# Six sums of squares of weights on VectorE, the high halves of GpSimd's splits on GpSimd, and a new order, in a fused attention and MLP kernel

## The chip, the cores and the metric

The kernel runs on one core of a Trainium2 chip. The metric is the device time of one execution in microseconds, taken as the median of several runs. The profiler also records one execution with a trace of every engine: TensorE (PE, with its weight loads PEld), VectorE (DVE), ScalarE (ACT), GpSimd (POOL) and SyncE (SP), which here only issues transfers.

## The reference, cut to what matters

```python
xn = _layernorm(A_x)                                  # 2048 tokens x 512
return x + _A_ref(xn, wq, wk, wv, wo, beta) + _B_ref(xn, w1, b1, w2, b2)

def _A_ref(x, ...):            # 32 heads of 16, 4 segments of 512 tokens
    q, k, v = x @ wq, x @ wk, x @ wv
    for s in range(4):
        a_dot = softmax(qs @ ks^T * scale + causal mask) @ vs
        a_mem = (phi(qs) @ M) / (phi(qs) @ z + 1e-6)   # phi(t) = t + 1 if t > 0, else exp(t)
        o = g * a_mem + (1 - g) * a_dot
        M += phi(ks)^T @ vs ; z += sum(phi(ks))
    return o @ wo

def _B_ref(x, ...):
    return gelu(layernorm(x) @ w1 + b1) @ w2 + b2      # 512 -> 1792 -> 512
```

## The kernel before

All large products are made in three f16 matmuls instead of one f32 matmul: each operand is split into a high half (the value, scaled and rounded to f16) and a low half (what rounding left over), and the products high x high, high x low and low x high are added in PSUM (`split3`, L480). A weight's scale is a power of two that is found on the chip from the weight's sum of squares. So each group of weights ("qk" is the first group of heads of wq and wk, "QK" the other three groups, "v", "1a" and "2a" the first halves of w1 and w2, "1b" and "2b" the second halves, "o" is wo) goes through four steps before TensorE can use it:

- `w_load` (L252 to L280): transfers into the place where the f16 halves will stand later, or into a borrowed tile (`pt`, `acc`, `oT`, `rc`, `ame`). All are issued on SyncE.
- `w_square` (L311): one ScalarE activation for each piece, which squares it and leaves the row sums in a column of `am`.
- `w_scale` (L326, L343 to L357): TensorE adds the row sums over the partitions by a matmul with `ones`; ScalarE takes a root through Ln and Exp (L320, L321), and VectorE cuts it to a power of two and inverts it.
- `w_split`: each 128x512 piece is split either the "V" way (ScalarE writes the high half, L366, and VectorE the low half, L367) or the "G" way (GpSimd scales the piece in place, L369, ScalarE copies it to f16 as the high half, L370, GpSimd subtracts the two for the low half, L371). The table `SPLIT` says which piece goes which way; 21 pieces go the G way.

The work is cut into 16 items of one segment and one group of 8 heads. For each item: the projections of k and q (`T`, L480, then L514 to L530), which go through DRAM (`kd`, `qd`) into stacked tiles `kst` and `qst`; row maxima of the logits (`M`: matmuls L621, VectorE L628; `R` writes them out to DRAM and back into `qst`); exponentials (`S`: matmuls L661, ScalarE L666, the causal mask on GpSimd L675); the product with v (`pv`, L690); normalisation (`O`, L698 to L726); the memory terms (L536 to L607). The MLP is 16 steps: hidden products (`D`, L480 with w1s, brought out by L756), gelu (`G`, L763), the split of the result (`H`, L770 on GpSimd, L771 on ScalarE, L772 on GpSimd) and the second product (`e`, L797, added by L803). `out` (L815, L818) is the last projection. There are also 14 `warm` steps of eight matmuls of `ones` with itself (L828), whose results are used by nothing.

No scheduler decides the order: every engine runs its own instructions in program order, and the program order is written out. `streams()` lists the steps of each kind in sequence, and the string `ORDER` names, letter by letter, which stream gives the next step. `BANKS` gives each new PSUM tile its bank in the same way. Both strings were found by a search.

Of the kernel before, what the change touches and what calls it, by code (L numbers as in the profile page):

```python
# [56 lines left out]
def streams():  # L57
# [31 lines left out]
    for m in PARTS:  # L89
# [10 lines left out]


ORDER = (
    "aatcucuccvavtctveecttcetcuvaactvuvtaatcattavdtubcwwvccfwxxcxwxyxyxxgyhxcoxxvwxofooowcvwzyzoiyyiazgyyziiynzoiiys"
    "ppAnziiniicvzvcniiooAzmAihiiopzqqiqcivpqjpqjijqqijizqjiqqjiiAwszBzoAskkkkmjiAojoijsoAijAqjqjasAfoAopgkkkkpjpjqq"
    "jlpoolojjjooilihAAkkkkpaiqqiqijqjqqijqjiqjqjisBfgpiiqkkkkmpliqqiooiqpBlqoBopohijjiojiijpolsjiqaqajqiqiqqiiqapka"
    "kmkktspaqijqiqjqiqajqbqajopijjgBfopkkkBkjjjlooooBlhjjjolqiqqiipkkkkjiqqijqqjjiqiqjjqiqiqiBkkkkmpliilfnplimpngrr"
    "mrjjponijqjqjinjipiskmkkmkaiijrijjoojiqsjqqjiqiiiqqkkkkihlqlfmlogojqjqjqqjjasoojmkkkkmqjiqjqjjaojjpipmooisikkkk"
    "lpilhiofmgoooqiqpppqiqiqqqiiiqqpsosmoiqqiiqiqppsslooijqjojijojijoiaakkkkmpaijqjqjaqqqjiqqjiqjqiikmkkakbqiaqqahl"
    "olfqjjojqmjgjjoolmmkkkkmhjjoojjiitjiojiippkkkkliiilnfnimpligniinipmrrijjrsijqjqiqjiqjqiipkmkkksiqjqijqjqjiqjqii"
    "qjqikmpkkkiprlqsphlfojmjgopjjlojpjoomokmkkkqiqisjojiqisjqiqijqqijqhiqqiiqjsqiiqppmkkkkilalofomqpgopaoooospmlajq"  # L110
    "qqjqqjqjqiiqiqqqjqiqqipipooooiijooppoiaakkkkmajiqpisqqjiqjqjaiqaqhjqqqjqaaqmkkkkbjlfoljqjmjgojjqolmkkkkmmjjjooj"
    "jioijoiiippkpkkkiinliifniiilnnimlgrpmjjrmjjjrrijikkpskkiqqijqiqijqqjiqjiqjqiqjiqiispqkpkskksqilqoplfojmjgjjjpoo"
    "oojolmkkkkiqjiqpsjiqiqijqjqiqijqjiqiqiqiiqqkksmkpikplolfjjqmjgjjjoooooklpkmkkjiiopjqiqijqjiqpjqiqijqiqqiqiiqikk"
    "pspkkqiplpoooopljjjqqqjqjjqooolkpskmkpkmqqqpqjpjqqqjqjqpqqjqjqqqkmkkkqlllqqqqqqqqqrrrr"
)

BANKS = (
    "012345670123457063571265407321640573216405732164053271640527163054271630542713605427105472105427105472105472015"  # L120
    "470251407251405712470512470512470536124075631254076340125637123756123576132576132576132576132576135402761350427"
    "163054273106542736574326574326537425632754632574631072456310724563071245360712453620731620731067203617621073621"
    "073621073621037621037621037261702361475023671540263701524603175246031746013746013713460713471630471630463714067"
    "314056723410523674105236741052367410527410527410527410527410527140352671450326475103264751023674523674523647253"
    "647236547236475264735264107532410765324107265431067512043675120436751204736152047361520473615270346150312750317"
    "250317253107250371257013275027135027134650132754062751340621375460376054370567403056374065374065307645307645307"
    "642153076241076241076241076253410762534621075346210754316024310264310432610432610324610324612403246013752640163"
    "754207156437120564371205647312056473120564731206547321065473265104723607423460273460273642073642073642051736420"
    "157642031765420316750316705315631705630157630157630157306173504621357462017345620147536210436024136024316403216"
    "403216403216403216740536740536740536740536271406"  # L130
)


# [14 lines left out]
def infini_mixer_kernel(ctx: ExitStack, tc: tile.TileContext, x, wq, wk, wv, wo, beta, w1, b1, w2, b2, out):  # L148
    nc = tc.nc
    V, A, G, T, Q = nc.vector, nc.scalar, nc.gpsimd, nc.tensor, nc.sync  # L150
# [136 lines left out]
    def w_square(m, k):  # L287
        if m in ("qk", "QK"):
            w, g = part(m, k)
            r, junk, to = piece(w, g), WT[w][:, 1], am[:, NG * "kq".index(w) + g:NG * "kq".index(w) + g + 1]  # L290
        else:
            to = am[:, AM[m] + k:AM[m] + k + 1]
            a = m[0]
            if m == "1a" and k == 2:
                r, to = b1t, am[:, 16:17]
            elif m[1:] == "a":
                r = flat(a)[:, 1024 + 1792 * k:2816 + 1792 * k]
            elif m[1:] == "b":
# [12 lines left out]
        A.activation(junk.bitcast(BF)[:, :r.shape[1]], r, AF.Square, accum_out=to)  # L311

    def floor2(dst, src):
# [45 lines left out]
    def w_split(m, n):  # L359
        w, c = part(m, n)  # L360
        s = qkcol(1, "kq".index(w), c) if w in "kq" else \
            col({"v": SV, "o": SO, "1": S1, "2": S2}[w] + (m[1:] == "b"))
        r = piece(w, c)
        h, l = WT[w][:, c, 0, :], WT[w][:, c, 1, :]
        if SPLIT[m][n] == "V":
            A.activation(h, r, AF.Copy, scale=s)  # L366
            V.scalar_tensor_tensor(l, r, s, h, op0=OP.mult, op1=OP.subtract)  # L367
        else:
            G.tensor_scalar(r, r, s, 0.0, op0=OP.mult, op1=OP.add)  # L369
            A.activation(h, r, AF.Copy)  # L370
            G.tensor_tensor(l, r, h, op=OP.subtract)  # L371

    wqs, wks, wvs, wos, w2s = (WT[m] for m in "qkvo2")
# [487 lines left out]
    def once(kind, n, make):  # L861
# [49 lines left out]
```

## Time and profile before

| | |
|---|---|
| median of 3 runs | 695.24 us (695.22 to 695.28) |
| the profiled execution, its time | 694.85 us |
| its span, first to last instruction | 693.1 us |
| mean granted TensorE clock | 0.995 |
| busy: PE / DVE / ACT / POOL | 678.7 / 535.4 / 522.7 / 347.2 us |
| ScalarE busy, 10 to 40 us from the start | 29.09 of 30 us |
| TensorE busy, 20 to 30 us | 5.41 of 10 us |

Times in the profile are counted from the first instruction of the span. A row of a timeline gives the start, the duration and the engine, then the line, the operation, what is written and read, and in brackets the idle time of the engine before it with what ended that idle time. A row of the windows view gives the length of a stretch, the busy time of PE, PEld, DVE, ACT and POOL in it with their numbers of instructions, the granted TensorE clock as a share of the full one, the share of the DMA engines and GB/s.

### The profile page before, as it was taken

What the parts mean: (1) busy time and instruction counts of PE and PEld (TensorE: products, weight loads), DVE (VectorE), ACT (ScalarE), POOL (GpSimd) and SP (SyncE); (2) the same over time, 40 slices, a digit from 0 to 9 for tenths busy, and PEclk for the clock granted to TensorE, in tenths of its full rate; (3) what the DMA queues carried; (4) which work ended last, traced back from release to release, by engine and by line L of the source; (5) the groups of instructions that cost most, each with busy time, mean ns of one, the idle gap of its engine ahead of it and who ended that gap; (6) DMA issues with size and microseconds to landing.
All of it is one profiled execution on the core that took longest, in us unless ns stands there. A gap on an engine that the chain in (4) does not pass through costs nothing.

```text
span 693.1 us, 16949 instructions
## 1 busy us (share of the span) xinstructions
PE 678.7 (98%) x6359; PEld 395.7 (57%) x6359; DVE 535.4 (77%) x1695; ACT 522.7 (75%) x1013; POOL 347.2 (50%) x533
## 2 busy tenths in 40 slices
PE   7799999999999999999999999999999999999997
PEld 6465556576654555566554456567564456656653
DVE  4499978897795887998798786888678595969442
ACT  5989898878795659857795697757795687778870
POOL 5276768365624425664334445454362546455752
PEclk9899999999999999999999999999999999999999
DMA  9984222420204213431113224231120416140101
GB/s 272 283 238 136 64 63 63 108 62 14 84 10 115 87 44 74 100 71 33 51 45 92 63 72 99 63 93 33 31 80 24 132 18 152 18 108 3 18 1 61
DMA packets 51790, 55.12 MB, mean 80 GB/s; under 512 B 4782, under 2 KB 40636, under 8 KB 51708
## 3 DMA queue, kind: packets, MB, share of 16 engines
q1 hardware_dynamic: 49404, 49.84, 25.3%
q0 software_dynamic: 2304, 4.20, 3.7%
q8 instruction: 50, 0.82, 0.5%
q14 instruction: 32, 0.26, 0.1%
HBM read 36.99 MB, written 17.04 MB: 78 GB/s over the span
## 4 chain that ended last, share of the span: by engine, by line
PE 78%; ACT 10%; POOL 4%; DVE 3%; issue 2%; DMA 1%; SPq 1%; POOLq 0%; ACTq 0%; DVEq 0%
PE ps L480 33%; PE ps L797 16%; PE ps L690 10%; PE ps L815 6%; PE ps L661 5%; PE ps L621 5%; ACT pt L666 2%; DVE ps L628 2%; PE ps L571 2%; PE ps L499 1%; ACT hT L763 1%; ACT hT L771 1%; SPq L252 1%; POOL w1s L371 1%; DMA pt<-in_A_wk_dram 1%
## 5 line engine op out<-in xcount | busy, mean ns | idle before, releaser
L628 DVE CUSTOM_DVE_ANT_0 ps<-ps,mask 128x512 f32<-128x512 f32 (+3 forms) x512 | 233.8, 522 | 16.1 <-PE ps L621 14.9
L666 ACT ACTIVATE pt<-ps,qkcs 128x512 f32<-128x512 f32 (+1 forms) x384 | 206.1, 624 | 35.3 <-PE ps L661 33.5
L797 PE MATMUL ps<-w2s,hT 64*128 64x512 f16 x1344 | 176.7, 376 | 0.2
L480 PE MATMUL ps<-xnT,w1s 128*128 128x256 f16 x1344 | 157.8, 273 | 0.0
L675 POOL TENSOR_SCALAR_AFFINE_SELECT pt<-pt 128x256 f32<-128x256 f32 x256 | 99.1, 414 | 92.0 <-ACT pt L666 91.0
L480 PEld LDWEIGHTS <-w1s 128*128 128x128 f16 x1344 | 127.3, 98 | 29.1 <-issue 11.3
L772 POOL TENSOR_TENSOR hT<-hh,hT 128x512 f16<-128x512 f32 x64 | 67.8, 1059 | 82.8 <-ACT hT L771 81.0
L797 PEld LDWEIGHTS <-hT 64*128 64x128 f16 x1344 | 76.3, 94 | 50.7 <-issue 6.0
L690 PE MATMUL ps<-pt,vt 128*32 128x512 f32 (+3 forms) x1024 | 77.3, 435 | 0.1
L756 DVE SCALAR_TENSOR_TENSOR hT<-ps,sc,sr 128x256 f32<-128x256 f32 x112 | 52.1, 478 | 27.2 <-PE ps L480 27.0
L628 DVE DVE_READ_ACCUMULATOR2_ANT mc<- 128x1 f32 x512 | 70.6, 138 | 0.0
L661 PE MATMUL ps<-qst,kst 50*128 50x512 f16 (+3 forms) x512 | 67.5, 298 | 0.3 <-ACT pt L666 0.2
L621 PE MATMUL ps<-kst,qst 48*128 48x256 f16 (+3 forms) x512 | 67.1, 297 | 0.5
L771 ACT ACTIVATE hT<-hh 128x512 f16<-128x512 f32 x64 | 36.6, 572 | 33.4 <-POOL hh L770 32.9
L690 PEld LDWEIGHTS ps<-pt,vt 128*32 128x32 f32 x1024 | 31.3, 109 | 42.4 <-issue 30.8
L770 POOL TENSOR_SCALAR hh<-hT,sc 128x512 f32<-128x512 f32 x64 | 41.8, 653 | 26.6 <-ACT hT L763 24.9
L720 POOL TENSOR_TENSOR nN<-nN,oT 128x512 f32<-128x512 f32 x16 | 20.3, 1267 | 61.3 <-DVE oT L546 61.3
L763 ACT ACTIVATE hT<-hT,b1t 128x256 f32<-128x256 f32 x112 | 46.4, 495 | 0.2
L480 PE MATMUL ps<-xnT,wqs 128*128 128x512 f16 x192 | 45.6, 389 | 0.0
L480 PE MATMUL ps<-xnT,wks 128*128 128x512 f16 x192 | 44.3, 379 | 0.0
L480 PE MATMUL ps<-wvs,xnT 128*128 128x512 f16 x192 | 44.0, 380 | 0.1
L815 PE MATMUL ps<-wos,oT 128*128 128x512 f16 x192 | 43.2, 380 | 0.6 <-POOL oT L726 0.6
(217 smaller groups left out, 890.0 us busy)
## 6 DMA issues: line engine op xcount, KB each, us to landing
kd<-hl SPq DMA_DIRECT2D x48, 128.0 KB
qd<-hl SPq DMA_DIRECT2D x48, 128.0 KB
kst<-kd SPq DMA_DIRECT2D x32, 192.0 KB
qst<-qd SPq DMA_DIRECT2D x32, 192.0 KB
acc<-in_A_x_dram SPq DMA_DIRECT2D x16, 256.0 KB
acc<-in_B_b_dram POOLq DMA_DIRECT2D x16, 256.0 KB, 4.1
out_dram<-acc SPq DMA_DIRECT2D x16, 256.0 KB
xt<-in_A_x_dram SPq DMA_DIRECT2D x14, 256.0 KB
```

The lines of the kernel that those rows point to most:

```text
L480: T.matmul(p, wsl(ws, k, a), xsl(xs, k, b), start=s0 and i == 0, stop=s1 and i == 3 * n - 1)
L621: T.matmul(p[:, o:o + n], stk[i, 0][r, t, P * qb:P * qb + P], stk[i, 1][r, t, :n], start=True, stop=True)
L628: V.tensor_tensor_reduce(p[:, o:o + n], p[:, o:o + n], mask[:, 512 - n:], 1.0, -3e38, OP.add, OP.max, mc[:, 16 * b + 4 * t + qb:16 * b + 4 ...
L661: T.matmul(p[:, o:o + n], stk[i, 1][r, t, P * kb:P * kb + P], stk[i, 0][r, t, P * kb:], start=True, stop=True)
L666: A.activation(e[:, OFF[kbs[0]]:OFF[kbs[0]] + o], p[:, :o], AF.Exp, scale=qkcs[:, 1, i % NG:i % NG + 1])
L675: G.affine_select(v, v, pattern=[[0, 2], [1, P]], compare_op=OP.is_ge, fill=0.0, base=0, channel_multiplier=-1)
L690: T.matmul(p[32 * c:32 * c + 32, P * kb:], vt[s, kb][:, 4 * g + c, 16 * odd:16 * odd + 32], pt[i, 2 * c + odd][:, OFF[kb]:OFF[kb] + LEN[kb ...
L756: V.scalar_tensor_tensor(hz[:, fi, :], p[:, :256], col(F1 + fh), srow[hs][:, own], op0=OP.mult, op1=OP.mult)
L763: A.activation(z, z, AF.Gelu_apprx_tanh, bias=b1t[:, FH * (j % 2) + f:FH * (j % 2) + f + 1])
L772: G.tensor_tensor(hT[:, z, 1, :], t, hT[:, z, 0, :], op=OP.subtract)
L797: w = T.matmul(pes[j][a], hTs[fh][r, fi, u, P * a:P * a + P], w2s[r, fo, v, :], start=n == 0 and m == 0, stop=fi == FH - 1 and m == 2, ski ...
L815: T.matmul(p, o[:, u, P * b:P * b + P], wos[:, g, v, :], start=i == 0, stop=i == 3 * NG - 1)
```

## The change

Three things are edited. Six squares, named in a new set `SQV`, are made on VectorE by one multiply-and-add instruction each: the three wq pieces of "QK", the second piece of "v", and the second of the two large pieces of "1a" and of "2a". For the last three the throw-away product goes to the place of wo's first pieces. In the G way of a split GpSimd now makes the high half itself, from the unscaled piece, and then scales the piece in place and subtracts as before; ScalarE has no part in it any more. And `ORDER` and `BANKS` are new strings, searched again; the streams, the tiles and the number of steps are the same.

```diff
+SQV = {("QK", 1), ("QK", 3), ("QK", 5), ("v", 1), ("1a", 1), ("2a", 1)}
...
 ORDER = (
-    "aatcucuccvavtctveecttcetcuvaactvuvtaatcattavdtubcwwvccfwxxcxwxyxyxxgyhxcoxxvwxofooowcvwzyzoiyyiazgyyziiynzoiiys"
+    "acceauuacevcttvtuvvcvttutvttcaaataatavcwccctweccudtxxcvctfxbxvcysyxxwxghvcywxxcwyycvxoxyyywwfgyzooooozsiiizznzo"
...
@@ w_square
+        if (m, k) in SQV:
+            if m != "QK":
+                junk = WT["o"][:, 0:2].rearrange("p n a c -> p (n a c)")
+            V.tensor_tensor_reduce(junk.bitcast(BF)[:, :r.shape[1]], r, r, 1.0, 0.0, OP.mult, OP.add, to)
+            return
         A.activation(junk.bitcast(BF)[:, :r.shape[1]], r, AF.Square, accum_out=to)
@@ w_split
         else:
+            G.tensor_scalar(h, r, s, 0.0, op0=OP.mult, op1=OP.add)
             G.tensor_scalar(r, r, s, 0.0, op0=OP.mult, op1=OP.add)
-            A.activation(h, r, AF.Copy)
             G.tensor_tensor(l, r, h, op=OP.subtract)
```

Below, a line of the changed kernel stands 1 to 6 higher than the same line before (L480 is L486, L343 is L349, L311 is L317, the new VectorE square is L315).

TensorE, from the end of the first k projection (`wks`) to the start of the first q projection (`wqs`); `am` holds the row sums of squares and `rat` a ratio of the layer norms. Before:

```order
L480 LDWEIGHTS wks
L480 MATMUL ps_393<-xnT,wks 128x512
L343 MATMUL ps_416<-am,ones 128x1 x2
L343 MATMUL ps_431<-am,ones 128x1 x2
L345 MATMUL ps_431<-am,ones 128x1
L480 LDWEIGHTS wqs
L480 MATMUL ps_453<-xnT,wqs 128x512
```

Now:

```order
L486 LDWEIGHTS wks
L486 MATMUL ps_399<-xnT,wks 128x512
L439 MATMUL ps_424<-ident,rat 128x128 x4
L349 MATMUL ps_430<-am,ones 128x1 x2
L351 MATMUL ps_430<-am,ones 128x1
L349 MATMUL ps_457<-am,ones 128x1 x2
L486 LDWEIGHTS wqs
L486 MATMUL ps_468<-xnT,wqs 128x512
```

The scale sums of "1a" (two L343 and the L345, now L349 and L351) stand in front of the q projection in both; those of "v" come after them now instead of ahead, and the transposes of `rat` have moved behind the k projection.

ScalarE, from the squares of wv to the first root for "1a" (`fa`). Before:

```order
L311 ACTIVATE wvs,am<-wvs 128x1024
L311 ACTIVATE wvs,am<-pt 128x1024
L370 ACTIVATE wks<-wks 128x512
L514 ACTIVATE hl<-ps_393 128x512
L517 ACTIVATE phk<-ps_393,qksc 128x512
L320 ACTIVATE fa<-ps_416,sc 128x1
L321 ACTIVATE fa<-fa 128x1
L311 ACTIVATE w1s,am<-w1s 128x1792 x2
L311 ACTIVATE w1s,am<-b1t 128x14
L366 ACTIVATE wvs<-wvs,sc 128x512
L320 ACTIVATE fa<-ps_431,sc 128x2
```

Now:

```order
L317 ACTIVATE wvs,am<-wvs 128x1024
L372 ACTIVATE wqs<-wqs,qksc 128x512
L317 ACTIVATE w1s,am<-w1s 128x1792
L520 ACTIVATE hl<-ps_399 128x512
L523 ACTIVATE phk<-ps_399,qksc 128x512
L317 ACTIVATE w1s,am<-b1t 128x14
L440 ACTIVATE sr<-ps_424 128x512
L326 ACTIVATE fa<-ps_430,sc 128x2
```

One square of wv, one of w1, the copy of a high half (L370) and a split of wv (L366) are gone from the stretch, and the remaining square of w1 now stands ahead of the two activations (L520, L523) that bring out the k projection.

More of the change, by code (lines that the diff above doesn't have):

```diff
@@ L102 @@
 ORDER = (
-    "aatcucuccvavtctveecttcetcuvaactvuvtaatcattavdtubcwwvccfwxxcxwxyxyxxgyhxcoxxvwxofooowcvwzyzoiyyiazgyyziiynzoiiys"
[L104 to L112, printed above, removed]
@@ L113 @@
-    "oojolmkkkkiqjiqpsjiqiqijqjqiqijqjiqiqiqiiqqkksmkpikplolfjjqmjgjjjoooooklpkmkkjiiopjqiqijqjiqpjqiqijqiqqiqiiqikk"
-    "pspkkqiplpoooopljjjqqqjqjjqooolkpskmkpkmqqqpqjpjqqqjqjqpqqjqjqqqkmkkkqlllqqqqqqqqqrrrr"
+    "acceauuacevcttvtuvvcvttutvttcaaataatavcwccctweccudtxxcvctfxbxvcysyxxwxghvcywxxcwyycvxoxyyywwfgyzooooozsiiizznzo"
+    "yiipzniizapniAspiiniiAAooAiiqizmpAohqicizqjvzqjiqiBvoopAijqjqijqiqiwzjqAkkkBkjizoAjqjqsijqjjafioaoppgAkkmkAkjqj"
+    "loopljAjjoooosljhiikkkpkisjqiqipAjqiqjqijqiqijqqijqiqqiBpmkkskkpifpgopopjqlqljooBolojihjijoiaaqaqjiqiiqpBakkkkm"
@@ new lines @@
+    "sqjqpqiqqijqjqiijaqbiqaoiaopiqjjpfgkkkkjjqqjlmohljfojqiolojiBpkkkkiqijBojiqqijqjijqiqjqiqiqiqiBppkkkklimlnnlgrs"
+    "rpjrmjqjjnijjniiispkmkakkjiopiqjiqiqjqiqjiqiqjiqqhjqiafrmskkkkjjlqolqjqjjqsmjgolkkkmmkmjjoojjjoojpiipskkkkiiloo"
+    "oolihmfpgoooppssiiqqiiqqqpiqqiiqqpmoqiippqqiqqiooijimotpijiloajjiojijoaiakakkkiqjqjqiqjqjqsaqjijqqqhakkkkbaqaqj"
+    "qjlmljfmajgojqjolkmkkkmjjmhoojijjiojipiipkkkklniilifmpignolaniiirrpiisipnrsjiqjiqqjijqjqiisqjqikkkmkmiqjiqjqjio"
+    "jiqjqjiqrsopmpkkkkjplqhlfjjmgjljpoooooopjmqkkkkmijqiqjqiqjiqqijqqiijqqiqjqiqikkkkpphilmioolfqimgopooooppssmjjqq"
@@ L115 @@
+    "jqqqqjjqqiqqiqjispqappqiiopooiiioloooaaskkkkmaiiqqpjiqqjqjiqqijjqaqjqhqakkkkmjaqqbalqjofljjmjlgooojmkkmkkjjomoj"
+    "joiijfijipkkkkpilipilnniimgplnfiiipprriiriipmrsjjjmnsijqjqjqiqipkkkkjiqqjiqjqjiqjiqjqiikkkklqqqlimgooopoolmjmjo"
+    "jjojqqjqiikpkkkiiqjqijqqjjiqiqjiqqijqiqiispkkkkospioplosplfjqmjgsjjooopjjqlomkkkkqjijiqsjijiqjiqjqiqiiqqiqqiiqp"
+    "piokkpikpkoloopljjqqjqjqjqjloooskpkpkkjqqpmqqjqqjqqjqpqqjjqqmpkkkkmlllqqqqqqqqqqqqrrrr"
 )
 BANKS = (
-    "012345670123457063571265407321640573216405732164053271640527163054271630542713605427105472105427105472105472015"
@@ L121 @@
[L121 to L130, printed above, removed]
+    "012345670124567302614305761230456127304561273045267130452761304527613045276130450613504613045613045614536013465"
@@ new lines @@
+    "016354013650413650413650413650134625701346251730462513704651236753612376513276251735612735612735612703456712034"
+    "561270345621703457603457603456705364750367450367450367450362714503271643271643162743162743621734621734612736412"
+    "743612743612743617243617243617520436715204367152403716524761576241572647152647152647126547126540731524607135240"
+    "671352640713526407135264035712640357126457126457126457126034571023640571263405172634051267340512673460573640573"
+    "640573640735640375640347056705364127503645127036415273604152736041273650412736054127360541273604512367521367152"
@@ new lines @@
+    "361576213572163527163527162375162375163270451327064532176405321763527163251763251372651236725316740253167402531"
+    "402531402531402531402543102567431025674310256743102675431657431764531764531765431657430251643702645163470215630"
+    "472156304576215730462157304621573046125730461257304612570436125703465703465706354706354673056473056473120564731"
+    "206547320651743651743516734571364356741356745163745163745163457203416720354167203167023167203167023162730162730"
+    "162730162307162307156247156247156247156243701563"
```

## The prediction

> **What bounds the kernel now.** I read the page first, for which engine is busy.
>
> ```profile
> PE 678.7 (98%) x6359; PEld 395.7 (57%) x6359; DVE 535.4 (77%) x1695; ACT 522.7 (75%) x1013; POOL 347.2 (50%) x533
> ```
>
> TensorE is busy 98% of the span. The matmuls that compute something are the same before and after, so a change that only shifts work between ScalarE, VectorE and GpSimd can gain only where TensorE waits. The windows view says where that is.
>
> ```profile
> core 0: us, PE busy (x) PEld busy (x) DVE busy (x) ACT busy (x) POOL busy (x), PEclk, DMA share, GB/s
> 0.00:6.60 6.60, 5.01 (x35) 4.00 (x36) 2.48 (x8) 1.28 (x1) 5.52 (x19) 1.00 0.61 197
> 0.00:21.80 21.80, 17.80 (x133) 13.83 (x134) 11.40 (x45) 14.54 (x35) 9.61 (x24) 1.00 0.98 277
> 0.00:26.70 26.70, 19.17 (x139) 14.92 (x139) 13.40 (x50) 19.38 (x44) 10.77 (x25) 0.96 0.99 295
> ...
> 24.00:26.00 2.00, 0.06 (x1) 0.06 (x1) 1.81 (x5) 1.97 (x4) 0.00 (x0) 0.68 1.05 389
> 26.00:28.00 2.00, 0.77 (x3) 0.68 (x4) 0.00 (x0) 1.97 (x5) 0.00 (x0) 0.50 1.11 335
> ...
> 40.00:80.00 40.00, 39.50 (x337) 22.13 (x336) 39.37 (x142) 36.17 (x71) 27.37 (x33) 1.00 0.56 163
> 80.00:640.00 560.00, 559.47 (x5407) 324.29 (x5407) 454.90 (x1452) 424.57 (x824) 276.29 (x432) 1.00 0.26 66
> ```
>
> From 80 to 640 us TensorE idles 0.5 us in all; between 24 and 28 us it works 0.8 of 4 us, while ScalarE is full. TensorE's and ScalarE's timelines name the work there:
>
> ```profile
> 9.60 0.38 PE L326 MATMUL ps<-am,ones 128*128 128x2 f32 x2 [1.31 <-ACT wqs L311]
> ...
> 15.30 1.91 PE L828 MATMUL ps<-ones 128*128 128x256 f16 x16
> 17.05 0.60 PE L466 MATMUL ps<-ident,nD 128*128 128x128 f32 x4
> ...
> 19.18 2.91 PE L480 MATMUL ps<-xnT,wks 128*128 128x512 f16 x12
> 21.93 0.71 PE L343 MATMUL ps<-am,ones 128*128 128x1 f32 x4
> 25.95 0.59 PE L343 MATMUL ps<-am,ones 128*128 128x1 f32 x2 [3.31 <-ACT w1s L311]
> 27.77 0.59 PE L343 MATMUL ps<-am,ones 128*128 128x1 f32 x2 [1.23 <-ACT w1s L311]
> ...
> 28.64 4.18 PE L480 MATMUL ps<-xnT,wqs 128*128 128x512 f16 x12
> ...
> 33.96 2.79 PE L480 MATMUL ps<-xnT,w1s 128*128 128x256 f16 x24
> 36.59 2.75 PE L480 MATMUL ps<-xnT,wks 128*128 128x512 f16 x12
> 39.18 5.40 PE L480 MATMUL ps<-xnT,w1s 128*128 128x256 f16 x48
> ```
>
> ```profile
> 22.62 0.58 ACT L514 ACTIVATE hl<-ps 128x512 f16<-128x512 f32 x1
> 23.10 0.68 ACT L517 ACTIVATE phk<-ps,qksc 128x512 f32<-128x512 f32 x1
> ...
> 24.10 1.70 ACT L311 ACTIVATE w1s<-w1s 128x1792 bf16<-128x1792 f32 x1
> ...
> 25.92 1.70 ACT L311 ACTIVATE w1s<-w1s 128x1792 bf16<-128x1792 f32 x1
> ...
> 27.74 0.21 ACT L311 ACTIVATE w1s<-b1t 128x14 bf16<-128x14 f32 x1
> ```
>
> TensorE waits 3.31 and 1.23 us for the two squares of "1a", one behind the other on ScalarE. The clock has fallen to 0.50 by then, and the q projection takes 4.18 us where `wks` at 36.59 takes 2.75.
>
> **The change part by part.** I sum to one point, the first hidden product (33.96 us): both orders put the same TensorE work ahead of it, but for the one warm-up more that comes early now.
>
> *When the weights land.* The loads up to the end of "1a" are 4 tiles of x, 8 pieces of wq and wk, wv and four 448 KB rows, 5,888 KB or 6.03 MB; 277 GB/s over 21.8 us is 6.04 MB. The first wk piece is the fifth of 256 KB, 1.31 MB, which 197 GB/s reach at 6.6 us; ScalarE's first square waits for it until 7.92 us:
>
> ```profile
> 7.92 0.63 ACT L311 ACTIVATE wks<-wks 128x512 bf16<-128x512 f32 x1 [5.82 <-DMA wks<-in_A_wk_dram]
> ```
>
> So a load is usable 1.3 us after its bytes: "1a" at about 23.1 us, and "2a" (7.86 MB; 295 x 26.7 is 7.88 MB) at 28.0 us. The change leaves the issue order of these as it is, so no square of "1a" can start before 23.1 us; ScalarE began at 24.10. That is the ceiling on the gain.
>
> *Up to the k projection.* The first wk and wq pieces are now ahead of two tiles of x, each 0.262 MB or 0.9 us at 295 GB/s, so the sum at 9.60 comes at 7.8. Behind it stand ten warm-ups of 0.88 us (16 matmuls from 15.30 to 17.05), four transposes of at most 0.6 (17.05) and two small sums of at most 0.38: at most 19.8 us if nothing waits, and about 0.5 more if the transposes of `nN` wait for ScalarE, which still has two squares that need the eleventh load ahead of them. I take 20.0, 0.8 later than now. This costs nothing: the projection (2.75 by the row at 36.59) and the `rat` transposes end at 23.1, no later than "1a" lands.
>
> *The squares of "1a".* ScalarE's takes 1.82 us by its spacing (24.10 to 25.92) and ends at 24.9. VectorE's has no row; the nearest is the same kind of instruction at L628, by shape:
>
> ```profile
> L628 DVE CUSTOM_DVE_ANT_0 ps<-ps,mask 128x512 f32<-128x512 f32 x128 | 86.8, 718 | 10.4 <-PE ps L621 10.1
> L628 DVE CUSTOM_DVE_ANT_0 ps<-ps,mask 128x128 f32<-128x128 f32 x128 | 36.9, 328 | 0.0
> ```
>
> 390 ns for 384 columns gives 328 + 1664 x 1.016 = 2.02 us, and about 0.14 for the read; ScalarE's 1.70 is the lower end and 2.5, with a wait for GpSimd (below), the upper. It ends near 25.3, beside ScalarE's. Behind its square ScalarE has the two activations of the k projection, 0.58 and 0.68 at most (L514, L517), and the 14-column square, 0.21: 26.4. The last sum and the "v" sums follow, 0.6 together (27.77 to 28.64 less one sum), and the q projection starts at 27.0 instead of 28.64: 1.6 us gained.
>
> *The q projection's clock.* TensorE stopped at 22.64 and the clock fell within the window 24 to 26 (0.68, so at about 24.7, 2.1 us later). In the new order the pause is 23.1 to 25.3, 2.2 us, then two short sums and another pause. By these rows the clock falls again and the projection takes 4.18 us; at full clock it would be 1.4 us less. I take the slow one. The Trainium skill ("TensorE: Matmul & The Clock Gate", Part 1) says that the clock is halved after an idle window of about 3.4 us that runs free of the kernel, so a 2.2 us pause need not halve it; the sum would then be larger by what the next wait leaves of 1.4 us.
>
> *From there to the hidden product.* Now 28.64 to 33.96 is 5.3 us; the same from 27.0 gives 32.3. Two things could be later: VectorE's "2a" square, from 28.9 behind the split of wqs to 31.0, so its sums at 31.4; and GpSimd's split of the first w1 piece.
>
> ```profile
> L369 POOL TENSOR_SCALAR w1s<-w1s,sc 128x512 f32<-128x512 f32 x7 | 5.3, 754 | 5.9 <-DMA kd<-hl 5.9
> L370 ACT ACTIVATE w1s<-w1s 128x512 f16<-128x512 f32 x7 | 4.4, 625 | 1.0 <-POOL w1s L369 1.0
> L371 POOL TENSOR_TENSOR w1s<-w1s 128x512 f16<-128x512 f32 x7 | 8.5, 1208 | 5.7 <-ACT w1s L370 5.7
> ```
>
> A split was 0.75, a wait for ScalarE's 0.63 and 1.2, some 2.6 us; it becomes 0.75 twice and 1.2, 2.7 (this operation has no row that writes f16; between L369's 0.75 and L371's 1.2 I take 0.75, as only the type written differs from L369). From the scale at 27.8 it ends at 30.5, before 32.3. So the hidden product starts at 32.3: **1.7 us** gained. Bounds: 0.5 (VectorE and GpSimd hold each other up for the 2 us of a whole square, and the split ends at 32.5 with sums behind it), 2.5 (full clock: 30.9, then limited by the 31.4 of the "2a" sums).
>
> *The other edits.* 21 copies of 0.625 us and six squares leave ScalarE, about 20 us; GpSimd gets 21 x 0.75 = 16 us, VectorE 8 us. TensorE covers all of it after 34 us (0.5 us idle from 80 to 640), so they count zero, unless VectorE, with 39.37 of 40 us, becomes the bound from 40 to 80 (rival below).
>
> *The order.* One late warm-up instead of two; in the chain of waits one is
>
> ```profile
> 157.88 0.98 PE ps L828 x8
> ```
>
> so **1.0 us** gained. And TensorE loses a little when it changes between matmuls that use the whole array and those on half of it or on column strips:
>
> ```profile
> 97.51 2.75 PE L480 MATMUL ps<-xnT,wqs 128*128 128x512 f16 x12
> 100.19 2.36 PE L690 MATMUL ps<-pt,vt 128*32 128x512 f32 x32
> ```
>
> Twelve 512-column matmuls take 2.68 us here, start to start, before the strips of L690, and 2.59 before more of their kind (36.59 to 39.18): 0.09. Counted over the orders the changes go from 232 to 222, **0.9 us** (0 to 1).
>
> Sum: 1.7 + 1.0 + 0.9 = 3.6. From the profiled 694.85 us this is 691.25; that execution lies 0.39 under the median of 695.24, so **691.6 us**.
>
> **The rivals.**
>
> *Full clock, and short waits gone.* A pause of 2.2 us does not halve the clock: 2.5 instead of 1.7. The 0.5 us that TensorE idles from 40 to 80 goes too, since ScalarE, 36.17 of 40 us there, is relieved. 4.9 us in all: 690.3. The skill's page above would have it so. Against it, the clock's row above.
>
> *The loads decide, and the new order waits elsewhere.* The gain at the start is its lower end, 0.5, the switches give nothing, and two new waits appear like that of the row maxima on their way through DRAM:
>
> ```profile
> 572.06 3.46 DMA qst<-md
> ```
>
> That leg alone takes 3.46 us and stands in the chain that ended last. At an estimated 0.4 us each, a ninth of it, 0.5 + 1.0 - 0.8 = 0.7: 694.5, no change.
>
> *Slower: GpSimd and VectorE block each other.* At 38 us a GpSimd scaling and two VectorE low halves overlap:
>
> ```profile
> 38.15 1.13 POOL L369 TENSOR_SCALAR w1s<-w1s,sc 128x512 f32<-128x512 f32 x1
> 37.92 0.81 DVE L367 SCALAR_TENSOR_TENSOR w1s<-w1s,sc 128x512 f16<-128x512 f32 x1 [0.39 <-ACT w1s L366]
> 38.65 1.17 DVE L367 SCALAR_TENSOR_TENSOR wqs<-wqs,qksc 128x512 f16<-128x512 f32 x1
> ```
>
> 1.13 against L369's mean of 0.754, 1.17 against 0.81 for the low half just ahead: about 0.4 each. The new GpSimd instruction stands where ScalarE worked before, and some 14 of the 21 fall between 30 and 90 us, where VectorE has no slack. If each costs VectorE 0.4 us and TensorE waits for all of it, 5.6 us: 697.2. It decides from 3.6 us on, 9 such meetings. The Trainium skill ("SBUF — State Buffer", Who interferes with whom) has it as a rule: a VectorE instruction with two SBUF inputs and a GpSimd instruction that reads SBUF exclude each other for a whole instruction. Against this rival: most of VectorE's work there is L628, with one input in PSUM, and it does not lengthen beside GpSimd:
>
> ```profile
> 58.31 0.73 DVE L628 CUSTOM_DVE_ANT_0 ps<-ps,mask 128x512 f32<-128x512 f32 x1
> 58.30 1.16 POOL L772 TENSOR_TENSOR hT<-hh,hT 128x512 f16<-128x512 f32 x1 [1.81 <-ACT hT L771]
> ```
>
> **How the numbers follow.** The forecast 0.47, full clock 0.20, no change 0.15, slower 0.13; 0.05 for a larger gain, as the whole order is new. 0.2%, 1.4 us, is about what a measurement can tell here: faster is below 693.85, slower above 696.6. Faster 0.47 + 0.20 + 0.05 = 0.72, same 0.15, slower 0.13. The range goes from 688.0, 2.3 below the full-clock case for waits that I did not count, up to 696.0, which takes in the no-change case; about 2 in 10 lie outside.
>
> **What would show it.** Right: squares of "1a" from 23 us on both engines, VectorE's near 2.0 us; the q projection at 27.0 and the first hidden product at 32.3; ScalarE near 503 us busy, GpSimd near 363, VectorE near 543. Wrong: the projection at 2.7 us (clock), VectorE's low halves above 1 us in large number with TensorE waiting between 40 and 80, or TensorE idle by more than 2 us between 80 and 640, which would be the new order's own.

## The result, and the profile after

| | before | changed | |
|---|---|---|---|
| median | 695.25 us (6 runs, 694.76 to 695.5) | 703.87 us (6 runs, 702.29 to 709.71) | ratio 1.014 (95% interval 1.0102 to 1.0178) |
| profiled execution, its span | 694.85, 693.1 us | 707.08, 705.3 us | 12.2 us more |

The kernel is slower by 1.4%, 8.6 us between the medians; forecast was 3.6 us faster. The profiled execution of the changed kernel is 3.2 us above its own median, which matters below. The page after:

```profile
PE 683.3 (97%) x6359; PEld 391.0 (55%) x6359; DVE 549.0 (78%) x1707; ACT 506.4 (72%) x980; POOL 369.8 (52%) x554
```

ScalarE, forecast at 503 us, is at 506.4; GpSimd and VectorE, forecast at 363 and 543, are 6.8 and 6.0 us above that. The windows view of the changed kernel, with the columns of the table shown for the kernel before:

```profile
0.00:26.70 26.70, 19.92 (x141) 14.86 (x141) 15.59 (x54) 12.28 (x28) 13.39 (x26) 1.00 0.93 276
24.00:26.00 2.00, 0.00 (x0) 0.00 (x0) 0.09 (x1) 0.15 (x1) 0.21 (x1) 1.00 1.02 345
26.00:28.00 2.00, 0.31 (x2) 0.31 (x2) 1.94 (x2) 2.00 (x3) 0.00 (x0) 0.90 1.04 386
40.00:80.00 40.00, 36.86 (x285) 21.77 (x285) 36.79 (x111) 25.12 (x50) 35.20 (x38) 0.96 0.49 144
80.00:640.00 560.00, 554.22 (x5345) 314.78 (x5342) 450.41 (x1424) 418.42 (x807) 281.15 (x438) 1.00 0.25 66
```

The pause of TensorE between 24 and 28 us is still there, only now ScalarE and VectorE are idle in its first half: they wait for the load. And TensorE, which idled 0.5 us in each of the last two stretches, idles 3.1 us from 40 to 80 and 5.8 us from 80 to 640. GpSimd is busy 35.20 of 40 us from 40 to 80, against 27.37. The timelines of the changed kernel name the work:

```profile
8.81 0.38 PE L332 MATMUL ps<-am,ones 128*128 128x2 f32 x2 [1.92 <-ACT wqs L317]
20.69 2.75 PE L486 MATMUL ps<-xnT,wks 128*128 128x512 f16 x12
27.69 1.01 PE L349 MATMUL ps<-am,ones 128*128 128x1 f32 x4 [3.81 <-ACT w1s L317]
30.25 4.79 PE L486 MATMUL ps<-xnT,wqs 128*128 128x512 f16 x12
35.83 1.65 PE L486 MATMUL ps<-xnT,w1s 128*128 128x256 f16 x12
52.11 1.05 PE L627 MATMUL ps<-kst,qst 48*128 48x384 f16 x5 [0.98 <-DVE hT L762]
...
25.85 1.70 ACT L317 ACTIVATE w1s<-w1s 128x1792 bf16<-128x1792 f32 x1 [5.34 <-DMA w1s<-in_B_w_dram]
53.49 1.48 ACT L317 ACTIVATE w1s<-w1s 128x1536 bf16<-128x1536 f32 x1 [6.95 <-POOL w1s L377]
...
25.91 2.02 DVE L315 CUSTOM_DVE_ANT_0 wos<-w1s 128x1792 bf16<-128x1792 f32 x1 [2.50 <-DMA w1s<-in_B_w_dram]
32.11 2.01 DVE L315 CUSTOM_DVE_ANT_0 wos<-w2s 128x1792 bf16<-128x1792 f32 x1
38.19 1.64 DVE L373 SCALAR_TENSOR_TENSOR w1s<-w1s,sc 128x512 f16<-128x512 f32 x1
...
30.96 0.69 POOL L375 TENSOR_SCALAR w1s<-w1s,sc 128x512 f16<-128x512 f32 x1 [6.76 <-DVE fa L359]
31.75 2.85 POOL L376 TENSOR_SCALAR w1s<-w1s,sc 128x512 f32<-128x512 f32 x1
34.69 1.47 POOL L377 TENSOR_TENSOR w1s<-w1s 128x512 f16<-128x512 f32 x1
```

Three things are to be seen. The two squares of "1a" run side by side, but start at 25.9 us, when the load is there. GpSimd's scaling at 31.75 takes 2.85 us beside VectorE's square of "2a" (32.11 to 34.12), where others of its kind, as at 37.04 us, take 0.69. And ScalarE waits 6.95 us for GpSimd at 46.5 us: the unused squares of "1b" are written over raw pieces of "1a" that GpSimd has not yet split.

The 12.2 us between the two profiled executions can be split in full. These are the windows from the first hidden product to the end, of before and then of the changed kernel:

```profile
33.96:693.10 659.14, 653.68 (x6195) 377.53 (x6192) 520.56 (x1639) 496.26 (x957) 333.88 (x505) 1.00 0.26 69
```

```profile
35.83:705.30 669.47, 655.44 (x6186) 371.50 (x6185) 525.53 (x1638) 486.93 (x937) 351.75 (x526) 1.00 0.25 67
```

The product starts 1.87 us later, TensorE idles 14.03 us behind it and not 5.46 (8.57 more), and its work takes 1.76 us longer; the clock was at 0.79 from 56 to 60 us. That sums to 12.20. What the experiments have to explain is above all the idle time.

### The profile page after: what moved, and what is told of

It reads as the page before. It is cut to its first block, busy times and chain, and to the rows that moved or that the text cites. A ratio compares the mean times of both kernels' runs of the same rounds, so it can differ in the third digit from the quotient of the medians.

```text
span 705.3 us, 16970 instructions
## 1 busy us (share of the span) xinstructions
PE 683.3 (97%) x6359; PEld 391.0 (55%) x6359; DVE 549.0 (78%) x1707; ACT 506.4 (72%) x980; POOL 369.8 (52%) x554
## 4 chain that ended last, share of the span: by engine, by line
PE 76%; DVE 6%; DMA 5%; ACT 5%; POOL 3%; issue 2%; SPq 2%; POOLq 0%; DVEq 0%; ACTq 0%
PE ps L486 33%; PE ps L803 16%; PE ps L696 9%; PE ps L821 6%; PE ps L627 5%; PE ps L667 5%; DVE ps L634 3%; ACT pt L672 2%; DMA qd<-hl 2%; PE ps L577 1%; DMA w1s<-in_B_w_dram 1%; DMA qst<-qd 1%; PE ps L505 1%; SPq L253 1%; POOL w1s L376 1%
## 5 line engine op out<-in xcount | busy, mean ns | idle before, releaser
L486 PE MATMUL ps<-xnT,w1s 128*128 128x256 f16 x1344 | 158.5, 274 | 1.9 <-DVE w1s L373 1.5
L486 PEld LDWEIGHTS <-w1s 128*128 128x128 f16 x1344 | 128.4, 98 | 30.1 <-issue 10.2
L803 PEld LDWEIGHTS <-hT 64*128 64x128 f16 x1344 | 72.6, 94 | 53.1 <-issue 3.6
L627 PE MATMUL ps<-kst,qst 48*128 48x512 f16 (+3 forms) x512 | 69.3, 299 | 3.8 <-DMA qst<-qd 1.5
L667 PE MATMUL ps<-qst,kst 50*128 50x384 f16 (+3 forms) x512 | 68.2, 298 | 2.5 <-DVE hT L762 1.0
L769 ACT ACTIVATE hT<-hT,b1t 128x256 f32<-128x256 f32 x112 | 46.5, 496 | 0.2
L486 PE MATMUL ps<-xnT,wqs 128*128 128x512 f16 x192 | 46.2, 392 | 0.0
L627 PEld LDWEIGHTS <-qst 48*128 48x128 f16 x512 | 28.6, 95 | 30.8 <-issue 14.6
L667 PEld LDWEIGHTS <-kst 50*128 50x128 f16 x512 | 26.7, 94 | 32.9 <-issue 16.4
L486 PE MATMUL ps<-xnT,wks 128*128 128x512 f16 x192 | 44.2, 380 | 0.0
L486 PE MATMUL ps<-wvs,xnT 128*128 128x512 f16 x192 | 43.8, 380 | 0.1
```

The costliest lines, as they stand in the source:

```text
L486: T.matmul(p, wsl(ws, k, a), xsl(xs, k, b), start=s0 and i == 0, stop=s1 and i == 3 * n - 1)
L627: T.matmul(p[:, o:o + n], stk[i, 0][r, t, P * qb:P * qb + P], stk[i, 1][r, t, :n], start=True, stop=True)
L667: T.matmul(p[:, o:o + n], stk[i, 1][r, t, P * kb:P * kb + P], stk[i, 0][r, t, P * kb:], start=True, stop=True)
L769: A.activation(z, z, AF.Gelu_apprx_tanh, bias=b1t[:, FH * (j % 2) + f:FH * (j % 2) + f + 1])
L803: w = T.matmul(pes[j][a], hTs[fh][r, fi, u, P * a:P * a + P], w2s[r, fo, v, :], start=n == 0 and m == 0, stop=fi == FH - 1 and m == 2, ski ...
```

## The experiments

Three theories stood first. **Theory 1**: the added GpSimd instruction and VectorE's work hold each other up, and the splits come late. **Theory 2**: the new order puts work in the wrong places. **Theory 3**: the new load order lets the weights land late. All ratios, with their 95% intervals, are to runs of the kernel before made alongside (their medians were 694.75 to 695.27 us); 0.1% is 0.7 us.

### The three edits apart

The change is two edits of instructions and one of the tables `ORDER` and `BANKS`. Each run below undoes one or two of them:

```diff
 # squares back on ScalarE
-SQV = {("QK", 1), ("QK", 3), ("QK", 5), ("v", 1), ("1a", 1), ("2a", 1)}
+SQV = set()
 # high halves back on ScalarE
-            G.tensor_scalar(h, r, s, 0.0, op0=OP.mult, op1=OP.add)
             G.tensor_scalar(r, r, s, 0.0, op0=OP.mult, op1=OP.add)
+            A.activation(h, r, AF.Copy)
 # old order: ORDER and BANKS of the kernel before
```

Both instruction edits, old order:

> The changed kernel's six sums on VectorE and its GpSimd high halves, with the order and bank tables of before. Theory 1 (the added GpSimd instruction of each split and VectorE's work hold each other up, so the chain of splits on GpSimd grows from 2.6 to 3.6 to 5.2 us a piece): it carries the loss, so 699 to 704 us. Theory 2 (the new order puts work in the wrong place whoever does it): the loss goes with the tables, so 693 to 696 us here. Theory 3 (loads land later and differ from run to run): as theory 2, and the runs lie within 1 us of each other.

New order alone:

> The new order and bank tables alone: all sums of squares on ScalarE, ScalarE makes the high halves. Theory 1: nothing was added to GpSimd, so 694 to 697 us. Theory 2: 700 to 705 us. Theory 3: slower by about 2 us, the later landing of the first w1 pieces and what follows from it (697 to 699 us), and with a spread of several us.

New order with GpSimd's high halves:

> The new order and GpSimd's high halves, with all sums of squares back on ScalarE. Theory 1: GpSimd's added instructions are there, VectorE's 2 us squares beside the splits are not: the first split of w1 takes about 3 us in place of 5.2, and the time lies between, 697 to 702 us. Theory 2: as the changed kernel, 702 to 705 us.

New order with the squares:

> The new order and VectorE's six sums, with ScalarE making the high halves again. Theory 1: GpSimd has two instructions for a piece, the last split of the first half of w1 ends some 6 us earlier than in the changed kernel, ScalarE's wait of 6.95 us for it goes, and the time is 695 to 699 us. Theory 2: 701 to 704 us.

Old order with the squares:

> The order of before and ScalarE's copies as before; only the six sums are on VectorE. Theory 1 (GpSimd's added instruction carries the 3.9 us that the old order loses with both edits): 693.5 to 696 us, and GpSimd's last split of the first half of w1 ends near 41.5 us as before. Rival (VectorE's squares carry it, since they delay VectorE's share of the splits and hold GpSimd up): 697 to 699 us.

Old order with GpSimd's high halves:

> The order of before and all sums on ScalarE; only GpSimd's high halves are changed. Theory 1: 697 to 700 us, with TensorE waiting for GpSimd's splits between 60 and 80 us as in the run with both edits. Rival (the squares carry it): 694 to 696.5 us.

| | old order | new order |
|---|---|---|
| neither | 695.25 us | 729.73 us, 1.0497 (1.0468 to 1.0526) |
| squares on VectorE | 695.69 us, 1.0006 (0.9996 to 1.0015) | 726.51 us, 1.0454 (1.0436 to 1.0471) |
| high halves on GpSimd | 697.90 us, 1.0037 (1.0023 to 1.0051) | 705.38 us, 1.0153 (1.012 to 1.0186) |
| both | 698.97 us, 1.0057 (1.0042 to 1.0072) | 703.87 us, 1.014 (1.0102 to 1.0178) |

In the old order the squares cost nothing that can be told from zero, the high halves 0.37%, both 0.57%, some 3.9 us. The new order adds 0.8% to that. So theory 1 and theory 2 each hold a part, theory 2 the larger. What none of the theories expected is the right column's upper half: the new order alone loses 34 us, and with the squares 31. The new order was searched for with splits that GpSimd makes by itself. With ScalarE's copy in the middle, the waits view of the new order alone, from 30 to 110 us (engine and line, what it waited for, us in all, times, longest), shows the two engines waiting for each other in turn, and TensorE for VectorE behind them:

```profile
POOL w2s L377 <- ACT w2s L376: 14.9, 5, 12.0
...
PE ps L627 <- DVE phk L536: 7.9, 1, 7.9
...
ACT w2s L376 <- POOL w2s L375: 7.5, 4, 2.3
```

From 34 to 110 us TensorE idles 15.0 us in this run, and its granted clock is 0.81 up to 80 us; the rest of the 34 us was not followed further. So an order and the instructions that it was searched for can't be priced apart from each other, and the instructions' price is read here in the old order.

### What the added instruction costs

In the run of the old order with the high halves alone, the first GpSimd split of w1 takes what was forecast, 2.7 us:

```profile
30.06 0.69 POOL L375 TENSOR_SCALAR w1s<-w1s,sc 128x512 f16<-128x512 f32 x1 [7.54 <-DMA kd<-hl]
30.84 0.69 POOL L376 TENSOR_SCALAR w1s<-w1s,sc 128x512 f32<-128x512 f32 x1
31.62 1.16 POOL L377 TENSOR_TENSOR w1s<-w1s 128x512 f16<-128x512 f32 x1
```

The later ones take longer. Two splits of w2 start 2.56 us apart in the kernel before (first two rows) and 3.14 apart here, where VectorE's low halves stand beside them and the first instruction takes 1.01 us:

```profile
46.95 0.69 POOL L369 TENSOR_SCALAR w2s<-w2s,sc 128x512 f32<-128x512 f32 x1
49.51 0.69 POOL L369 TENSOR_SCALAR w2s<-w2s,sc 128x512 f32<-128x512 f32 x1
...
52.70 1.01 POOL L375 TENSOR_SCALAR w2s<-w2s,sc 128x512 f16<-128x512 f32 x1
55.84 1.01 POOL L375 TENSOR_SCALAR w2s<-w2s,sc 128x512 f16<-128x512 f32 x1
```

With VectorE's squares too, the middle row of the first split is 2.34 us, and the split 4.7. VectorE pays as well. Its low halves of w1 (the groups view; after the bar the busy time and the mean ns) in the kernel before and in the old order with both edits, the latter with three of TensorE's waits:

```profile
L367 DVE SCALAR_TENSOR_TENSOR w1s<-w1s,sc 128x512 f16<-128x512 f32 x5 | 3.8, 756 | 4.2 <-ACT w1s L366 4.1
```

```profile
L373 DVE SCALAR_TENSOR_TENSOR w1s<-w1s,sc 128x512 f16<-128x512 f32 x5 | 5.7, 1136 | 0.9 <-ACT w1s L372 0.9
...
58.76 0.38 PE L627 MATMUL ps<-kst,qst 48*128 48x384 f16 x3 [0.88 <-DVE mc L634]
72.17 1.26 PE L486 MATMUL ps<-xnT,w1s 128*128 128x256 f16 x10 [0.65 <-POOL w1s L377]
77.75 0.39 PE L803 MATMUL ps<-w2s,hT 64*128 64x512 f16 x2 [0.63 <-POOL hT L778]
```

These are the longest of TensorE's waits there, on GpSimd and on VectorE. From 40 to 80 us it idles 3.34 us, against 0.50 in the kernel before: the greater part of the 3.9 us. Which of the two engines is late? VectorE waits 1.3 us in all between 44 and 87 us (**theory 5**: it is the bound there). Two runs took work from it: ScalarE writes zeros in place of three of its low halves, which are so left out. A third gave one of its splits to GpSimd, nothing left out.

```diff
 # less work for VectorE
+            if m == "2a":
+                A.activation(l, r, AF.Copy, scale=0.0)
+            else:
                 V.scalar_tensor_tensor(l, r, s, h, op0=OP.mult, op1=OP.subtract)
 # one more split on GpSimd
-SPLIT = {... "2a": "GVGVGVG", ...}
+SPLIT = {... "2a": "GVGVGGG", ...}
```

Old order, both edits, less work for VectorE:

> The old order with both edits (699.0 us); ScalarE writes zeros in place of the three low halves of w2's first half that VectorE made (line 373, 1.0 us each beside GpSimd), so those low halves are left out. Theory 5 (VectorE is the bound from 44 to 92 us, and what GpSimd's added instructions lengthen on it is the loss): its first wait of over 1 us comes 2.5 to 3.5 us earlier, 695.5 to 696.7 us. Rival (GpSimd's longer chain of splits is the bound): 698.5 to 699.3 us.

Kernel before, less work for VectorE:

> The same three low halves left out of the kernel before (0.75 us each on VectorE). Theory 5: VectorE's slack comes 2 us earlier than 87.4 us, 692.5 to 693.7 us. Rival (TensorE alone is the bound, busy 39.5 of 40 us from 40 to 80): 694.8 to 695.5 us.

Kernel before, one more split on GpSimd:

> The kernel before with one split of the first half of w2 on GpSimd and not on VectorE, nothing left out. Theory 5: VectorE has 0.75 us less to do, GpSimd's two instructions hold it up by up to 0.4 us: 694.2 to 695.0 us. Rival (GpSimd's chain, then 2.6 us longer, delays the next pieces): 695.5 to 697 us.

Measured: 698.95 us, 1.0054 (1.004 to 1.0067); 695.92 us, 1.0013 (1.0003 to 1.0022); 697.65 us, 1.0038 (1.0026 to 1.0051). Theory 5 falls: VectorE relieved by 2 to 3 us, at the price of three more instructions on ScalarE, gains nothing (the profiled execution of the first, 697.94 us, is the lowest of its four; the second is 0.13% slower, outside both expected ranges). In the first, TensorE's wait for VectorE at 58.76 us is gone, and the time stays; its waits for GpSimd behind 70 us stay as well. But one more split on GpSimd costs the kernel before 2.6 us, as long as such a split is. GpSimd is the engine without slack. The last subtraction of its sixth split of w1, in the kernel before, with one more split, and with both edits:

```profile
66.40 1.17 POOL L371 TENSOR_TENSOR w1s<-w1s 128x512 f16<-128x512 f32 x1 [0.74 <-ACT w1s L370]
```

```profile
69.33 1.16 POOL L371 TENSOR_TENSOR w1s<-w1s 128x512 f16<-128x512 f32 x1 [0.75 <-ACT w1s L370]
64.86 1.48 PE L480 MATMUL ps<-xnT,w1s 128*128 128x256 f16 x12 [0.38 <-POOL w1s L371]
```

```profile
70.96 1.15 POOL L377 TENSOR_TENSOR w1s<-w1s 128x512 f16<-128x512 f32 x1
```

The end of this split, the span and TensorE's idle time from 40 to 80 us, in the profiled executions of runs in the old order:

| | split ends | span | difference | TensorE idle |
|---|---|---|---|---|
| before | 67.57 | 693.1 | 625.5 | 0.50 |
| squares | 68.14 | 694.1 | 626.0 | 0.52 |
| before, less VectorE work | 68.53 | 694.2 | 625.7 | 0.45 |
| one more split on GpSimd | 70.49 | 696.2 | 625.7 | 1.93 |
| high halves | 70.51 | 696.3 | 625.8 | 2.58 |
| both, less VectorE work | 70.52 | 696.2 | 625.7 | 2.36 |
| both | 72.11 | 698.2 | 626.1 | 3.34 |

In the first three the split moves with the whole start and TensorE does not wait for it; in the last four TensorE waits for GpSimd's splits, and the time goes with them. So GpSimd, 68% busy from 40 to 80 us in the kernel before (27.37 of 40), was already just in time with its chain of splits: its idle time lay between its instructions, where it waited for ScalarE, 7.5 of 12.6 us for the copies of the high halves and most of the rest for the MLP's results.

### What the order costs

Up to about 90 us the new order's first 182 steps and the old order's first 180 are the same but for four, and up to about 200 us both have done the same 368. So one can be continued by the other, with the changed instructions throughout and the bank numbers renamed at the seam:

```diff
+ORDER = new_order[:182] + (old order without the steps already done)    # and the reverse; and [:368]
```

> The changed kernel's instructions; the new order for its first 182 items (to about 90 us), then the order of before for what is left. Theory 2a (the new order's price, 4.9 us beside the old order with the same instructions, is the sum of TensorE's short waits after 90 us, which come to about 5 us in the run with the moved unused squares): 699 to 700.5 us. Theory 2b (the price arises before 90 us): 703 to 704.5 us.

> The counterpart: the order of before for its first 180 items, then the new order. Theory 2a: 702.5 to 704 us, with TensorE's waits at 270 and 630 us for VectorE and for loads of queries as in the changed kernel. Theory 2b: 698.5 to 699.5 us.

> The new order for its first 368 items, then the order of before. Theory 2a: only the waits after about 200 us go (some 3 us): 700 to 701.5 us. Theory 2b: 703 to 704.5 us.

Measured: 701.66 us, 1.0094 (1.0077 to 1.0111); 702.99 us, 1.0119 (1.0104 to 1.0134); 702.54 us, 1.0105 (1.0088 to 1.0121). Against the old order with the same instructions (1.0057) the new start costs 0.37%, 2.6 us, and the new rest 0.62%, 4.3 us; both together would be 1.0156, within the interval of the changed kernel. These prices go by steps: in the first run's profile TensorE idles 2.62 us from 90 to 200 us, against 0.26 in the old order with both edits, so part of what the new start costs shows behind it, or is made by the seam, which these runs can't tell apart. The theory that placed all of it after 90 us was right on the larger part and missed the start; the third run, at 702.54 us, lies outside both theories' ranges, and its interval overlaps with the first one's. The old start with the new rest has the changed kernel's waits, which neither the kernel before nor the new start with the old rest has:

```profile
275.80 0.37 PE L667 MATMUL ps<-qst,kst 50*128 50x384 f16 x3 [1.03 <-DVE hT L762]
634.94 0.39 PE L627 MATMUL ps<-kst,qst 48*128 48x512 f16 x1 [0.80 <-DMA qst<-qd]
637.45 0.39 PE L667 MATMUL ps<-qst,kst 50*128 50x512 f16 x2 [0.34 <-DVE mc L634]
```

No single one is large. Four repairs were tried in the start of the new order:

```diff
 # junk_moved: unused squares of "1b" to the empty tile of wo
-            junk = WT[a][:, c:c + 2]
+            junk = WT["o"][:, 0:2] if m == "1b" else WT[a][:, c:c + 2]
 # w1_splits_together: in ORDER, two splits of "QK" and two of "2a" behind the last split of "1a"
 # loads_as_before: in ORDER, the second step ("X", 0, 1, 0) ahead of the first loads of wk and wq
 # new_order_sum_later: junk_moved, and in ORDER ("wf", "1b") behind ("M", 0, 4)
```

> The changed kernel, with the unused squares of the second half of w1 (line 317) written to the still empty tile of wo and not over the raw pieces that GpSimd splits last. Theory 1: ScalarE's wait of 6.95 us for GpSimd at 46.5 us goes, TensorE's wait at 52 to 58 us shrinks by 1 to 3 us, 701 to 703 us. If the wait had cover, 703.5 to 704.5 us.

> The changed kernel with four splits moved in its order: two pieces of wk and wq and the first two of w2 come behind the last split of the first half of w1, so GpSimd does the four pieces of w1 one after the other, as in the order of before. Theory 2 (the order costs its 5 to 6 us by the pieces put between them): the last of them ends near 47 us in place of 53.5, and the time is 699 to 702 us. If the order costs its time elsewhere: 703 to 706 us.

> The changed kernel with the second pair of x loads ahead of the first pieces of wk and wq, as before. Theory 3 (the new order of the first loads delays the first w1 pieces and makes the time vary): the squares of w1 start near 24.0 us in every profile, the runs lie within 1 us and the median is 701.5 to 703 us. If the order of these loads doesn't matter: 703 to 704.5 us with a spread of several us.

> The changed kernel with the unused squares moved (702.97 us), and the scale of the second half of w1 (line 321 on VectorE) four groups of maxima later, so VectorE does these while it waits 3.0 us for ScalarE's sums. Theory 5: VectorE is the bound here too until 92 us, TensorE's wait at 92 us moves forward by 1 to 2.5 us, 700.5 to 702 us. Rival: 702.8 to 703.5 us.

Measured: 702.97 us, 1.0113 (1.0098 to 1.0128); 703.72 us, 1.0126 (1.0111 to 1.0141); 705.04 us, 1.0145 (1.013 to 1.016); 702.67 us, 1.0108 (1.0094 to 1.0122). ScalarE's 6.95 us wait for GpSimd goes in the first, and in the second the last split of "1a" ends at 45.2 us and not 53.5; yet the medians are 0.9 and 0.15 us below the changed kernel's, the ratios 0.27% and 0.14%, and the intervals overlap with its own. What goes of TensorE's waiting with the first is 0.89 us, three short waits for the late squares at 56 to 58 us; ScalarE then waits 7.91 us for TensorE. So the wait of 6.95 us, the most striking row of the trace, was for the most part covered. Theory 3 falls: with the loads issued as before, nothing is gained (its four executions lie within 1.4 us, so they may have a part in the spread). In the last one the waits move on, from VectorE at 50 us to these:

```profile
65.49 0.50 PE L627 MATMUL ps<-kst,qst 48*128 48x384 f16 x6 [1.35 <-ACT vt L599]
71.08 0.55 PE L608 MATMUL ps<-vt,pkn 128*32 128x48 f32 x32 [1.08 <-DVE mhl L645]
91.22 1.05 PE L486 MATMUL ps<-xnT,w1s 128*128 128x256 f16 x8 [1.50 <-DVE w1s L373]
```

### The clock

In the run with the moved squares the granted clock falls to 0.50 right after three short waits of TensorE (windows view, clock in the third column from the right):

```profile
46.00:50.00 4.00, 2.42 (x16) 1.30 (x15) 3.97 (x8) 2.59 (x6) 3.82 (x4) 0.98 0.90 332
50.00:56.00 6.00, 5.86 (x17) 2.03 (x17) 5.21 (x21) 0.00 (x0) 5.46 (x8) 0.50 0.67 199
...
92.79 1.27 PE L486 MATMUL ps<-xnT,w1s 128*128 128x256 f16 x10 [1.50 <-DVE w1s L373]
```

**Theory 4**: that is the price of the new start. Two runs filled TensorE's pauses with idle matmuls on the `ones` tile, one in this kernel, one in the kernel before, where the prediction had placed its gain.

```diff
-... [("warm", n) for n in range(14)]
+... [("warm", n) for n in range(16)]    # 18 for the kernel before; the new steps stand in the pauses
```

> The changed kernel with the unused squares moved (as in the run junk_moved, 702.97 us), and sixteen more of the idle matmuls on the ones tile, eight ahead of each of the first two groups of the maxima (line 627), where TensorE waits 0.47, 0.23 and 0.97 us between 47.7 and 50.1 us. They take 2.1 us and cover 1.7. Theory 4 (those waits drop the granted clock to 0.50 from 50 to 57 us, and that costs more than the waits): the clock stays at 1.00 there, 700 to 701 us. Rival (the clock falls for another reason, or costs nothing): 703 to 703.8 us, with the clock at 0.50 as before.

> The kernel before, with 32 more idle matmuls: eight ahead of the sum for wv and 24 ahead of the sums for the first half of w1, in TensorE's pause from 22.6 to 28.6 us. Theory 4: the clock is 1.00 and not 0.50 from 26 to 32 us, the q projection takes 2.8 us and not 4.2, the first hidden product starts near 32.9 us in place of 33.96 and the time is 693.8 to 694.8 us. Rival (GpSimd's splits of w1 set what follows): the clock stays up and the time is 695 to 695.5 us.

Measured: 705.15 us, 1.0138 (1.0118 to 1.0158), 2.2 us above the unfilled run with overlapping intervals; and 698.47 us, 1.0044 (1.0029 to 1.0058), above both ranges. The first run's windows and its wait at 92 us:

```profile
46.00:50.00 4.00, 3.89 (x33) 2.92 (x31) 3.97 (x9) 1.66 (x6) 3.73 (x5) 1.00 0.98 363
50.00:56.00 6.00, 6.00 (x46) 3.81 (x45) 5.50 (x26) 2.30 (x4) 5.46 (x8) 1.00 0.63 184
...
92.93 1.27 PE L486 MATMUL ps<-xnT,w1s 128*128 128x256 f16 x10 [1.49 <-DVE w1s L373]
```

The clock stays up, and TensorE comes to the same wait, which ends at 92.93 and not 92.79: what it gained it lost again in other waits on the way, 1.08 us for VectorE at 70 us among them. Theory 4 falls. In the new start the time up to 93 us is set by the engines that TensorE waits for, so its own clock before that is not the price. The run with the later sum agrees: there the clock is 1.00 from 46 to 62 us without filling, and the median is 702.67 us.

In the kernel before the filled pause brings the first hidden product to 33.35 us, 0.6 earlier, but the clock falls all the same a little later:

```profile
22.00:28.00 6.00, 4.65 (x39) 3.75 (x38) 2.00 (x5) 5.91 (x12) 1.15 (x1) 1.00 1.07 367
28.00:34.00 6.00, 5.65 (x32) 3.24 (x32) 2.11 (x7) 5.97 (x11) 2.72 (x4) 0.72 0.70 207
```

Its ten executions lie between 695.49 (the profiled one) and 699.77 us. Why most of them are 3 us above the profiled one stays open; the trace shows only the good one. That one has a span of 693.8 us, 0.7 above the kernel before, though its hidden product is 0.6 earlier and its sixth split of w1 ends 0.6 earlier, at 66.96 us. So an earlier first hidden product, the point to which the prediction summed, did not make even this execution shorter.

## Why the prediction was wrong

**The landing of "1a"**, forecast at 23.1 us, was 25.85 in the profiled execution and 23.5 to 24.0 in the seven other profiles with the new start and the squares on VectorE. So the estimate from bytes and bandwidth was 0.4 to 0.9 us early, and this one execution was late by two more. The hidden product, forecast at 32.3, came at 35.83 here and at 32.5 to 34.6 in the others with the changed start and both instruction edits. In the two earliest, TensorE made two of its matmuls and then waited some 1 us for GpSimd's split, as in the run with the later sum:

```profile
32.53 0.38 PE L486 MATMUL ps<-xnT,w1s 128*128 128x256 f16 x2
33.90 1.26 PE L486 MATMUL ps<-xnT,w1s 128*128 128x256 f16 x10 [0.99 <-POOL w1s L377]
```

So the forecast gain of 1.7 us was there at best in small part.

**VectorE's square**, 2.02 us forecast, was 2.02. **The q projection's clock**, forecast low, was 0.50, and the projection took 4.79 us where 4.18 was forecast. In this execution the pause was longer than forecast; in the run with the moved squares it was 2.34 us, near the forecast 2.2, and the clock fell to 0.50 at 26 us as well, the projection taking 5.04 us. The Trainium skill ("TensorE: Matmul & The Clock Gate", Part 1) has an idle window of about 3.4 us; by the rows here less was enough. **A GpSimd split**, 2.7 us forecast, is 2.72 when VectorE leaves it alone, and later splits stood 3.14 us apart beside VectorE's low halves. The first was 5.2 here. The bound "0.5" had named that case, VectorE's whole square against it, and should have been the forecast: the square of "2a" and the first split were both due between 27.8 and 31.0 us by the prediction's own times.

**"TensorE covers all of it after 34 us, so they count zero"** is the step that failed first; the order's term, below, is the second. Of the forecast, 1.7 us of gain at the start and nothing for the rest of the instruction edits became 3.9 us of loss in the old order, and 1.9 us of gain by the order became some 5 us of loss. That TensorE was full from 80 to 640 us said that it never waited for the others, and not how near they came to letting it wait. GpSimd's chain of splits had no slack up to 67 us, as the run with one more split shows (2.6 us for 2.6). The high halves cost 0.37% in the old order, 2.6 us, and 3.9 us together with the squares. The rival that had GpSimd and VectorE block each other was right in sign and near in size (5.6 us), but it sought the slack on VectorE; lightening VectorE gained nothing. The Trainium skill's rule that it named ("SBUF — State Buffer", Who interferes with whom) agrees with the rows, 2.85 us for 0.69 beside a VectorE square of 2.01.

**The order**, forecast to gain 1.9 us from a warm-up and fewer switches, cost 2.6 us by its first 182 steps and 4.3 by the rest. I had priced what TensorE does in it and not when VectorE's and ScalarE's steps come in it. The test that the prediction gave for this, TensorE idle by more than 2 us between 80 and 640, came out at 5.8.

**What stays open**: which of the new order's many short waits would have to go to win back its 5 us (none of four repairs won more than 0.32%), and why the changed kernel's executions spread over 7 us where those of before spread over 1. No version here beats the kernel before; the old order with the squares alone equals it.

## What to carry to other kernels

A bound engine at 98% hides other engines' work only as far as they have slack, and busy shares don't show slack: an engine that is 68% busy in a chain of hand-overs may be just in time, and one test with one step more shows it at once. An order that was searched for a set of instructions belongs to that set: here the same order lost 34 us with the instructions of before and 9 with its own. The longest wait in a trace need not be the dearest; taking away 6.95 us of ScalarE's waiting gained 0.9 us by the medians, which is not clear of the noise.

## What was not expected of the hardware

The granted clock fell to 0.50 for 6 us after TensorE had been busy 2.42 of 4 us, with no single wait over 1 us, and it stayed at 1.00 where these waits were filled, so several short waits can do what one long pause does. When they do so is not settled: after the same three waits in the changed kernel's own profile, at 50 to 52 us, the clock stayed at 1.00 until past 58 us and three more short ones. And a GpSimd instruction that writes f16 took the same 0.69 us for 128x512 as one that writes f32, while beside a two-input VectorE instruction either took about 1.0 us and more, up to 2.85.
